# Full-width output tiles and a transposed remainder in a fused attention and FFN kernel

**What was changed.** In three of four token blocks the output projection is cut differently (512 columns per row tile, and the other 128 columns made transposed), and the order in which its pieces are mixed with the P·V work is a fixed list of names.

## The chip, the cores and the metric

One core of one Trainium2 chip. The metric is device time in microseconds (us). The time of a kernel is the median of its runs; "fast" is a state of a run in which the clock was not lowered, and all repeated runs here were fast (experiment 1 was run once, so its state is not known). Ratios are the mean time of one kernel's fast runs over the mean of the other's fast runs of the same rounds, so they are not quite the ratio of the medians that are quoted.

## The reference

```python
# x (1, 2048, 640); 32 heads of 192; the last 512 cache positions; all bfloat16
xn = layernorm(x)
q  = (xn @ wq)                         # (2048, 32*192), split in heads
p  = softmax(q @ k[last 512].T * 192**-0.5)
s  = (p @ v[last 512]) as (2048, 6144) @ wo      # (6144, 640)
g  = silu((silu(xn @ w_gate) * (xn @ w_up)) @ w_down)
out = x + s * g
```

## The kernel before

Tokens are handled in four blocks of 512 (`b` = 0 to 3), each of four row tiles of 128 tokens (`qt`). After an FFN part come 16 head pairs. Each pair has a phase of projections and scores, then a stretch in which P·V of this pair alternates with the output projection of blocks two steps back. Most matmuls (9,526 of 11,086 in the record) use only 64 of 128 rows: the contraction of 128 is split in a lower half `lo` and an upper half `hi`, whose matmuls run side by side in the array. They write different banks of PSUM (the memory that the matmuls write to) and exchange banks half way, with a small memset on GpSimd ("turn") as the synchronization.

The parts that matter, with cuts marked by `...`:

```python
    def wo_turn(st, i, qt, turn):            # half of one row tile: 6 matmuls of 320 columns
        ps = st["sc"]
        for j in range(3):
            for k, r in enumerate((lo, hi)):          # lower, upper, lower, upper ...
                n = k ^ turn
                m = nc.tensor.matmul(
                    ps[:, n, 0:HD], OTs[i][r, 3 * qt + j, :], pairs[i // NB]["wo"][r, j, n * HD : (n + 1) * HD],
                    start=(turn == 0 and j == 0), stop=(turn == 1 and j == 2), skip_group_check=True,
                )
                after(m, st)
        if turn == 0:
            turned(m, st)

    def wo_tile(i, qt):
        ...
        def second():
            sc = st["sc"]
            wo_turn(st, i, qt, 1)
            s_t = sacc[:, t, :].rearrange("p (n d) -> p n d", n=2)
            ...
                nc.vector.tensor_tensor(s_t, s_t, sc[:, :, 0:HD], ALU.add)
        return [first, second]

    def woven(i):                            # the order of one step of a stretch
        (a, b), (w, x, y, z) = (pv(i, 0), pv(i, 1)), (wo_tile(i - 2, qt) for qt in range(4))
        for part in (*a[:2], drop, w[0], *b[:2], w[1], x[0], *a[2:], x[1], y[0], *b[2:], y[1], z[0]):
            part()
        held.append(z[1])
    ...
    for pr in range(NPAIR):
        ... # projections and scores of the four blocks
        for b in range(NB):
            i = pr * NB + b
            if i < 2:
                two(pv(i, 0), pv(i, 1))
            ...
                woven(i)
            ...
            if b == 0 and pr + 2 < NPAIR:
                load_k(pr + 2)
            elif b == 1 and pr + 2 < NPAIR:
                load_wq(pr + 2)
            elif b == 2:
                load_wo(pr + 1)
    ... # last pair: P·V, last output projection, one store per row tile
```

All these loads, all DMA transposes and nearly all stores are issued from one queue, that of SyncE (SPq in the profile), in program order.

The softmax here doesn't subtract the row's maximum and nothing guards it: scores larger than these inputs give would overflow.

## Time and profile before

| | before |
|---|---|
| median, runs beside the changed kernel | 922.53 us (922.36 to 923.72, 6 runs) |
| span of the profiled execution | 920.66 us |
| TensorE busy | 99% of the span |
| period of a head pair, pairs 3 to 14 | 47.03 us, 12 times |

A word on reading. PE is TensorE's matmuls and PEld its weight loads; DVE is VectorE, ACT ScalarE, POOL GpSimd; SPq is SyncE's queue of DMA issues. In a group line the columns are line, engine, operation, output and inputs with their size, count, then busy time and mean duration of one, then the idle time before them. In a timeline a line is start, length, engine, line, operation and count, with idle time and what ended it in brackets; neighbours of one kind are run together. The timeline of SyncE's queue before:

```profile
905.17 4.04 SPq L670 DMA_DIRECT2D out_dram<-x_r  x8
909.30 7.95 SPq L670 DMA_DIRECT2D out_dram<-ob  x7
918.04 0.33 SPq L663 DMA_DIRECT2D out_dram<-ob  x1
```

Every row tile has a store of its own; the last issue is 1.6 us after the last group of matmuls starts (916.45 us).

The view of TensorE's waits lists only two, both before the first head pair, and both for DVE (total us, times, longest).

```profile
PE gu L225 <- DVE zero_t L174: 1.2, 1, 1.2
PE tp L326 <- DVE xn L262: 0.2, 1, 0.2
```

### The profile page before, as it was taken

The numbers are of one execution on the slowest core, as the hardware profiler recorded it, in microseconds if no ns is written. First come the engines' busy times: TensorE is split into PE (matmuls) and PEld (weight loads), VectorE is DVE, ScalarE is ACT, GpSimd is POOL, SyncE is SP. The second block draws the span as 40 slices with busy tenths as digits, with TensorE's granted clock in tenths as the row PEclk, the third lists the DMA queues.
The fourth block names the chain that finished last, engine by engine and source line by source line (L and its number), as shares of the span: only waits on it lengthen the run. The fifth ranks groups of instructions, "written<-read, shape, count | busy, mean of one in ns | idle before, by whom it ended". The sixth has DMA issues, their size and how long they took to land.

```text
span 920.7 us, 25767 instructions
## 1 busy us (share of the span) xinstructions
PE 914.6 (99%) x11086; PEld 625.9 (68%) x11102; DVE 575.8 (63%) x847; ACT 474.6 (52%) x850; POOL 101.9 (11%) x390
## 2 busy tenths in 40 slices
PE   9999999999999999999999999999999999999998
PEld 5455556575858585868686767676777777676666
DVE  6343331467676767676766667676767676767656
ACT  4222222556464646565556565655555555556461
POOL 0000000000000000000000000000000000002978
PEclk9999999999999999999999999999999999999999
DMA  9330510045644444435536262635271717163524
GB/s 308 64 75 18 110 35 1 1 78 89 92 74 85 82 83 83 79 87 70 97 62 104 60 108 53 113 48 119 44 122 36 130 37 126 31 129 86 130 62 142
DMA packets 243762, 77.18 MB, mean 84 GB/s; under 512 B 224576, under 2 KB 243648, under 8 KB 243648
## 3 DMA queue, kind: packets, MB, share of 16 engines
q1 hardware_dynamic: 243216, 75.14, 41.9%
q8 instruction: 87, 1.43, 0.7%
q10 hardware_dynamic: 432, 0.39, 0.2%
q14 instruction: 27, 0.22, 0.1%
HBM read 39.45 MB, written 2.62 MB: 46 GB/s over the span
## 4 chain that ended last, share of the span: by engine, by line
PE 98%; POOL 0%; DMA 0%; DVE 0%; issue 0%; POOLq 0%; ACT 0%; DVEq 0%
PE mm L440 22%; PE sc L576 19%; PE sc L454 18%; PE mm L479 16%; PE sc L277 11%; PE mm L299 6%; PE sc L548 2%; PE mm L531 2%; POOL ob L636 0%; PE gu L277 0%; PE mm L548 0%; PE mm L312 0%; DMA x_t<-in_A_x_dram 0%; PE sc L479 0%; PE sc L531 0%
## 5 line engine op out<-in xcount | busy, mean ns | idle before, releaser
L458 ACT ACTIVATE p_t<-sc 128x1024 bf16<-128x1024 f32 x254 | 253.0, 1023 | 128.2 <-PE sc L454 128.2
L445 DVE TENSOR_REDUCE qT<-mm 128x512 bf16<-128x1024 f32 x189 | 231.1, 1223 | 95.3 <-PE mm L440 92.8
L509 ACT ACTIVATE O_b<-mm,r 128x192 bf16<-128x192 f32 x486 | 165.0, 422 | 180.8 <-issue 156.3
L440 PE MATMUL mm<-xnT,wq_p 64*128 64x512 bf16 x1890 | 240.2, 376 | 0.0
L601 DVE TENSOR_TENSOR sacc<-sacc,sc 128x640 f32<-128x640 f32 x200 | 164.2, 821 | 87.0 <-PE sc L576 87.0
L576 PE MATMUL sc<-wo_p,OT_b 64*128 64x320 bf16 x2592 | 217.3, 296 | 0.0
L454 PE MATMUL sc<-qT,khat 64*128 64x512 bf16 x1524 | 198.2, 376 | 0.0
L479 PE MATMUL mm<-V_p,p_t 64*128 64x193 bf16 x3520 | 186.4, 242 | 0.0
L479 PEld LDWEIGHTS <-p_t 64*128 64x128 bf16 x3584 | 162.9, 93 | 12.1
L440 PEld LDWEIGHTS <-wq_p 64*128 64x128 bf16 x1890 | 105.7, 94 | 93.4 <-issue 0.5
L576 PEld LDWEIGHTS <-OT_b 64*128 64x128 bf16 x2592 | 140.4, 94 | 21.4
L454 PEld LDWEIGHTS <-khat 64*128 64x128 bf16 x1536 | 85.9, 94 | 79.8
L564 POOL MEMSET turn_t<- 128x1 f32 x328 | 32.5, 99 | 691.9 <-PE mm L479 469.7
L285 DVE TENSOR_TENSOR hT<-sc,sg 128x512 bf16<-128x512 f32 x46 | 31.7, 691 | 83.7 <-ACT sg L284 83.7
L284 ACT ACTIVATE sg<-sc 128x512 bf16<-128x512 f32 x46 | 27.3, 597 | 73.4 <-PE sc L277 71.9
L277 PE MATMUL sc<-xnT,wg_sb 128*128 128x512 bf16 (+1 forms) x248 | 59.5, 353 | 0.7
L277 PE MATMUL sc<-xnT,wu_sb 128*128 128x512 bf16 (+1 forms) x259 | 60.2, 354 | 0.1
L299 PE MATMUL mm<-wd_sb,hT 128*128 128x320 bf16 x384 | 56.6, 299 | 0.0
L498 DVE RECIPROCAL r<-mm 128x4 f32<-128x4 f32 x124 | 22.6, 182 | 46.9 <-PE mm L479 36.1
L299 PEld LDWEIGHTS <-hT 128*128 128x128 bf16 x384 | 37.6, 98 | 18.9
L277 PEld LDWEIGHTS <-wu_sb 128*128 128x128 bf16 x285 | 27.1, 98 | 26.9 <-issue 0.2
L277 PEld LDWEIGHTS <-wg_sb 128*128 128x128 bf16 x285 | 27.1, 98 | 22.7
(69 smaller groups left out, 374.9 us busy)
## 6 DMA issues: line engine op xcount, KB each, us to landing
wo_p<-in_A_wo_dram SPq DMA_DIRECT2D x16, 480.0 KB, 4.4
K_p<-in_A_k_cache_dram SPq DMA_DIRECT2D x32, 192.0 KB, 3.3
V_p<-in_A_v_cache_dram SPq DMA_DIRECT2D x32, 192.0 KB, 3.0
wq_p<-in_A_wq_dram SPq DMA_DIRECT2D x64, 80.0 KB, 3.0
wq_p<-in_A_wq_dram SPq DMA_DIRECT2D x16, 160.0 KB, 3.4
x_r<-in_A_x_dram SPq DMA_DIRECT2D x16, 160.0 KB, 4.7
x_t<-in_A_x_dram SPq DMA_DIRECT2D x14, 160.0 KB, 3.0
OT_b<-O_b SPq DMA_TRANSPOSE x124, 3.0
```

Of the source, the lines that this page charges most:

```text
L277: nc.tensor.matmul(out, w_sb[:, c, f * P : (f + 1) * P], xnT[:, c, qc], start=(c == 0), stop=(c == NC - 1),)
L285: nc.vector.tensor_tensor(hTs[b][:, f, :], u, sg[:], ALU.mult)
L299: nc.tensor.matmul(dn[:, 0:HD], hTs[b][:, f, ti * P : (ti + 1) * P], wd_sb[:, f, cols], start=(f == 0), stop=(f == NF - 1),)
L440: nc.tensor.matmul(q_ps[:, h, :], pairs[pr]["wq"][r, c, j * P : (j + 1) * P], xnT[r, c, b * 512 : (b + 1) * 512], start=(c == 0), stop=(c ...
L445: nc.vector.reduce_sum(qTs[i][:, j, :], q_ps[:, :, :].rearrange("p h n -> p n h"), axis=AX.X)
L454: nc.tensor.matmul(sc[:, h, :], khat[r, j, ks], qT[r, j, :], start=(j == 0), stop=(j == 2))
L458: nc.scalar.activation(p_t[:, :, :], sc[:, :, :], ACT.Exp, scale=scale)
L479: m = nc.tensor.matmul(acc[:, k, h * 256 : h * 256 + Dh + 1], Ps[i][kc][r, h, qt * P : (qt + 1) * P], V_p[r, kc, h, 0 : Dh + 1], start=(p ...
L509: nc.scalar.activation(O_b[:, qt, h, :], a_k[:, h, 0:Dh], ACT.Copy, scale=r[:, k, h, :])
L564: st["turn"] = nc.gpsimd.memset(turn_t[:], 0.0)
L576: m = nc.tensor.matmul(ps[:, n, 0:HD], OTs[i][r, 3 * qt + j, :], pairs[i // NB]["wo"][r, j, n * HD : (n + 1) * HD], start=(turn == 0 and j ...
L601: nc.vector.tensor_tensor(s_t, s_t, sc[:, :, 0:HD], ALU.add)
```

## The change

The intent: pieces of 512 columns instead of 320, so fewer instructions for the same columns. A row tile of 640 output columns becomes 512 columns (`MAIN`), two row tiles sharing one PSUM buffer, and the last 128 columns of a whole block are made the other way round: the weights stand still, the 512 tokens move, and the result is transposed. Sums, gate and x of those columns are kept transposed too; three DMA transposes turn them back at the end. Block 3 stays as it was. A list of names sets the order of the units.

```diff
+    def wo_rest(ps, i, r=slice(0, P), first=True, end=True):
+        for j in range(3):
+            nc.tensor.matmul(
+                ps.rearrange("p (t q) -> p t q", q=P), pairs[i // NB]["wo"][r, j, MC:D],
+                OTs[i][:, :, :].rearrange("p (t j) q -> p j t q", j=3)[r, j, :, :],
+                start=(first and j == 0), stop=(end and j == 2),
+            )
...
+    def wo_units(i):
...
+        def rest():
+            sc = sc_tile()
+            for n, r in enumerate((lo, hi)):        # three lower, then three upper
+                wo_rest(sc[:, n, :], i, r)
+            for n in range(2):
+                add_sum(pr + n, s_t[:, b, :], sc[:, n, :])
+        if b == MB:
+            return [unit([(qt, cols) for cols in HALVES]) for qt in range(4)]
+        return [unit([(2 * h + k, MAIN) for k in range(2)]) for h in range(2)] + [[rest]]
...
-    def woven(i):
-        (a, b), (w, x, y, z) = (pv(i, 0), pv(i, 1)), (wo_tile(i - 2, qt) for qt in range(4))
-        for part in (*a[:2], drop, w[0], *b[:2], w[1], x[0], *a[2:], x[1], y[0], *b[2:], y[1], z[0]):
-            part()
-        held.append(z[1])
+    FIRST = """0a0 0b0 0a1 0b1 0e0 1b0 1a0 1b1 2a0 1a1 2w0 2a1 2w1 2x0 2b0 2x1 3x0 2b1 3x1 3a0 2y0 3a1
+        3b0 3y0 3w0 3b1 3w1"""
+    LATER = """0a0 0b0 0y0 0x0 0a1 0x1 0w0 0b1 0w1 1x0 1a0 1x1 1b0 1w0 1a1 1w1 1z0 1b1 1z1 1y0 2b0 1y1
+        2y0 2b1 2x0 2a0 2x1 3w0 2a1 3w1 2w0 3a0 2w1 3b0 3a1 3y0 3x0 3b1 3x1"""
...                                                # end of the kernel
-        for k in range(2):
-            wo_last(b, 2 * q2 + k, G)
+        last_rows(b, slice(2 * q2, 2 * q2 + 2), G, sc_tile)
+        if q2:
+            last_rest(b, V if b else G, mm_tile if b else sc_tile)   # ends in a DMA transpose
         if more:
             pv_full(i + more[0], more[1])
+        if q2:
+            store_block(b)                                           # 640 KB in one store
+    last_rest(2, V, sc_tile)
...
```

In a name such as `2w1`, 2 is the step, `a` and `b` are P·V units, `w`, `x`, `y`, `z` output units (`y` is the transposed piece in blocks 0 to 2, `e` a projection), and the last digit the half of the unit. The down-projection of the FFN was cut in the same way.

## The prediction

> **What bounds the kernel now.** I read the page first (engine shares, chain, groups), then the timeline inside one head pair, then the waits.
>
> ```profile
> PE 914.6 (99%) x11086; PEld 625.9 (68%) x11102; DVE 575.8 (63%) x847; ACT 474.6 (52%) x850; POOL 101.9 (11%) x390
> ...
> PE 98%; POOL 0%; DMA 0%; DVE 0%; issue 0%; POOLq 0%; ACT 0%; DVEq 0%
> ...
> L440 PE MATMUL mm<-xnT,wq_p 64*128 64x512 bf16 x1890 | 240.2, 376 | 0.0
> L576 PE MATMUL sc<-wo_p,OT_b 64*128 64x320 bf16 x2592 | 217.3, 296 | 0.0
> L454 PE MATMUL sc<-qT,khat 64*128 64x512 bf16 x1524 | 198.2, 376 | 0.0
> L479 PE MATMUL mm<-V_p,p_t 64*128 64x193 bf16 x3520 | 186.4, 242 | 0.0
> ```
>
> TensorE is busy 99% of the span, it is 98% of the chain that ended last, and its large groups were never idle before an instruction (the last column is 0.0). But busy time of pipelined matmuls is no rate, so I took starts from the timeline: first in the stretch of projections and scores, then in the stretch where P·V and the output projection alternate.
>
> ```profile
> 404.46 0.83 PE L454 MATMUL sc<-qT,khat 64*128 64x512 bf16 x6
> 405.11 1.26 PE L440 MATMUL mm<-xnT,wq_p 64*128 64x512 bf16 x10
> 406.19 1.48 PE L454 MATMUL sc<-qT,khat 64*128 64x512 bf16 x12
> ```
>
> ```profile
> 477.62 0.85 PE L479 MATMUL mm<-V_p,p_t 64*128 64x193 bf16 x16
> ...
> 478.29 0.99 PE L576 MATMUL sc<-wo_p,OT_b 64*128 64x320 bf16 x12
> 478.59 0.10 POOL L564 MEMSET turn_t<- 128x1 f32 x1 [0.57 <-PE mm L479]
> 478.91 0.82 DVE L601 TENSOR_TENSOR sacc<-sacc,sc 128x640 f32<-128x640 f32 x1 [0.66 <-PE sc L576]
> ...
> 479.10 0.85 PE L479 MATMUL mm<-V_p,p_t 64*128 64x193 bf16 x16
> ```
>
> The first column is the start. The matmuls use 64 of 128 rows, so a lower-half and an upper-half matmul run together; I call such a pair a slot. Ten 512-column matmuls take 406.19 - 405.11 = 1.08 us: 216 ns a slot. Sixteen of 193 columns take 478.29 - 477.62 = 0.67 us: 83 to 84 ns. Twelve of 320 take 479.10 - 478.29 = 0.81 us: 135 to 136 ns.
>
> Now one head pair in slots: projection 60 and scores 48 of 512 columns, P·V 128 of 193, output projection 96 of 320: 108 x 0.216 + 128 x 0.083 + 96 x 0.136 = 23.3 + 10.6 + 13.0 = 46.9 us. The view of stretches puts the period, start of one pair's P·V phase behind the next one's projections included, at:
>
> ```profile
> 442.45:489.48 47.03, 47.03 (x669) 33.92 (x664) 32.62 (x46) 26.80 (x49) 2.38 (x24) 1.00 0.45 81
> ```
>
> 47.03 us at full granted clock. So there is no waiting left inside a pair, and any order of the units can at best win about 0.1 us a pair. The first FFN part is as dense: in the chain, twelve down-projection matmuls take 69.21 - 67.58 = 1.63 us, 136 ns each.
>
> ```profile
> 67.58 1.63 PE mm L299 x12
> 69.21 2.16 PE sc L277 x10
> ```
>
> **What the Trainium skill says.** "TensorE: Matmul & The Clock Gate", section "Back-to-back issue gap", gives N/2.4 + 2.5 ns for a warm matmul of N columns: 82.9, 135.8 and 215.8 ns for 193, 320 and 512. The trace agrees with all three. Of that, only the 2.5 ns belongs to the matmul and not to its columns. The same page, section "The mechanism", says of row-tiled matmuls that their starts and ends are monotone in program order, "strict FIFO, no reordering"; only weight loads are pulled ahead. "PSUM — Partial Sum Buffer", section "Engine vs sequencer instructions", also says that matmuls start and complete in program order, weight loads apart. The trace of before neither shows nor contradicts it: lower and upper half alternate there in every case, so nothing ever stood blocked in front of a free half. "TensorEngine Tiling (Array Packing)", section "Gotcha 1: PSUM Pressure", says that different row tiles cannot use one PSUM bank at once. That explains the turn memsets on POOL, and why the new 128-column piece has two banks and two adds.
>
> **The change part by part.**
>
> Removed. In blocks 0 to 2 an output row tile was two pieces of 320 columns; it is one of 512, and the remaining 128 columns are made transposed, with 512 tokens as the moving side. Per pair and block, 24 slots of 320 become 12 + 3 slots of 512. Both are 7680 columns, so only 9 x 2.5 = 22 ns are saved; times 48 (16 pairs, 3 blocks) 1.1 us. FFN down: 96 matmuls of 320 become 60 of 512 in three blocks, 3 x 36 x 2.5 ns = 0.3 us. One hole of some 0.08 us in the first pair's P·V stretch may close. Sum: -1.4 us.
>
> Added on TensorE. The transposed piece is emitted by a helper that is called once per half with the three contraction steps inside it. The changed kernel's instruction order therefore has three lower-half matmuls, then three upper-half ones; all other row-tiled work alternates. That order gives 164 places where a matmul follows one of the same half, and before had none: four in each of 41 pieces (pairs 0 to 12 with 3 blocks, pair 13 with 2; the others use all 128 rows). With in-order starts the lower ones start at 0, 216 and 432 ns, and the first upper one only after the third, at about 452, though its half has been free since about 20 ns. So the upper half falls 432 ns behind. Before a piece the lower half may already run ahead, but by no more than one 193-column slot less the 20 ns between starts, 63 instead of 20 ns, so from the second piece on 432 - 43 = 389 ns are lost. 41 x 0.389 + 0.04 = 16.0 us. Nothing hides it, since TensorE is the path.
>
> Moved, beside the path. DVE adds per block were 4 x 0.82 = 3.3 us; now two of 1024 columns and two of 512. For 1024 I take the 1.22 us of the q sums (same PSUM width), for 512 the 0.69 us of the FFN gate: 3.8 us. Over three blocks +1.6 us on 32.6 us of DVE in a period of 47: no bound. ScalarE does the same work. Twelve more DMA transposes of x fall in the FFN part, where the DMA row shows idle slices; three transposes of output come before the block stores at the end.
>
> Waits that the new order could bring, as distance against need. A turn needs the matmul's tail of 0.16 us (its 242 ns less the slot of 83), the memset of 0.10 and the semaphores, about 0.4 us; the shortest distance between the two turns of a unit is one half of a P·V unit, 0.66 us. A score buffer behind the transposed piece needs 2 x 0.69 + 0.2 = 1.6 us and has three units, 1.96 us. The tightest P·V buffer (second unit of step 0, reused in step 1) needs the reciprocal 0.18, four ScalarE copies 1.4 and 0.3 of tails, 1.9 us, and has 2.1. All fit, the last narrowly; the lag makes the distances longer. So +0.
>
> Sum: 922.8 - 1.4 + 16.0 = 937.4, less rounding: 937.3 us (+1.6%).
>
> **Rivals.**
> (1) The halves queue separately, and the upper three run beside the lower three. For it: the order of the units was tuned with a model, which should have priced such a loss. Against it: both page statements, and that one instruction stream feeds both halves. It would make 922.8 - 1.4 = 921.4 us.
> (2) One matmul per half can wait outside the queue: then only the third blocks, 216 ns less per piece, 41 x 0.17 = 7 us lost: 928.5 us.
> (3) A new wait binds: the P·V buffer above, or DVE behind the two adds. At 0.1 us for each of 4 blocks in 14 pairs it would be 5 us more. Against it: the distances above.
> (4) The end: block 2's store of 640 KB waits for the last output transpose and stands ahead of the final row tiles in the queue. Stores of 160 KB land in 1.9 us and the transposes in some 3, and the last matmuls of block 3 run some 6 us after block 2's: hidden, or up to 2 us.
>
> **Range and chances.** In-order starts get 0.8, with 936 to 939.5 from small waits and the end; partial blocking 0.08, separate queues 0.12. The range 928 to 940.5 holds the first two. Two per cent of 922.8 is 18.5 us: the gain ever possible is 1.4, so faster is 0.01; slower than 941.2 needs in-order starts and some 4 us of rivals 3 or 4: 0.05.
>
> **What would show each step.** Starts of the six matmuls of one transposed piece: 0, 216, 432, then 452, 668, 884 if in order; pairs 20 ns apart if rival 1 holds. The period should be 47.03 + 3 x 0.389 - 0.07 = 48.1 us; 46.95 under rival 1. The slots should keep 83, 136 and 216 ns. FFN should end 0.3 us earlier. New PE waits on DVE or ACT would show rival 3; a longer stretch from the last matmul (4.0 us now) to the end rival 4. The prediction is wrong if the period stays at 47 or grows by a cause other than these six matmuls.

## More of the kernel before

```profile
194.45 2.60 SPq L512 DMA_TRANSPOSE OT_b<-O_b  x2
197.23 1.22 SPq L102 DMA_DIRECT2D K_p<-in_A_k_cache_dram  x2
198.50 3.39 SPq L512 DMA_TRANSPOSE OT_b<-O_b  x2
201.98 2.81 SPq L113 DMA_DIRECT2D wq_p<-in_A_wq_dram  x5
204.90 3.44 SPq L512 DMA_TRANSPOSE OT_b<-O_b  x2
```

In the first stretch, transposes of P·V outputs (which the output projection needs as its weights) share the queue with loads for later pairs.

## The result and the profile after

| | before | after |
|---|---|---|
| median | 922.53 us | 925.94 us (925.50 to 927.23, 6 runs) |
| ratio, after over before | | 1.0036, 95% interval 1.0024 to 1.0049 |
| span of the profile | 920.66 us | 923.99 us |

The changed kernel is correct and 0.4% slower. By the threshold of 2% that is "same", the class that the prediction gave 0.94, but 937.3 us and the range from 928 to 940.5 were wrong. From the page of the changed kernel: busy times, the chain by engine, and groups.

```profile
PE 914.2 (99%) x10172; PEld 538.7 (58%) x10193; DVE 594.7 (64%) x844; ACT 473.8 (51%) x841; POOL 91.0 (10%) x302
...
PE 97%; DMA 1%; SPq 1%; DVE 0%; issue 0%; POOLq 0%; POOL 0%; DVEq 0%
...
L619 PE MATMUL sc<-wo_p,OT_b 64*128 64x512 bf16 (+1 forms) x1608 | 180.5, 345 | 0.4 <-DMA OT_b<-O_b 0.4
L499 PE MATMUL mm<-V_p,p_t 64*128 64x193 bf16 x3520 | 179.2, 242 | 0.0
...
L632 DVE TENSOR_TENSOR s_m<-s_m,sc 128x1024 f32<-128x1024 f32 x82 | 100.2, 1221 | 49.3 <-PE sc L619 43.0
...
L632 DVE TENSOR_TENSOR s_t<-s_t,sc 128x512 f32<-128x512 f32 x82 | 56.3, 686 | 18.2 <-PE sc L587 16.8
```

There are 914 fewer matmul records (11086 and 10172; a few are missing, the weight loads fall by 909), TensorE is still the path, and the adds last what was predicted. New in the chain are 1% of DMA and 1% of SyncE's queue. The stretches of one head pair (start and end, its length, busy time of TensorE, of its weight loads, of DVE, ACT and POOL, then the granted clock):

```profile
491.54:538.50 46.96, 46.96 (x613) 29.08 (x611) 33.97 (x45) 26.83 (x49) 1.79 (x18) 1.00 0.46 82
```

46.96 us, 0.07 *less* than before, where the prediction had 48.1. So the predicted lag of the transposed pieces is not there. The timeline around one such piece:

```profile
480.39 0.82 PE L587 MATMUL sc<-OT_b,wo_p 64*128 64x512 bf16 x6
...
481.04 0.84 PE L499 MATMUL mm<-V_p,p_t 64*128 64x193 bf16 x16
...
481.33 1.40 DVE L632 TENSOR_TENSOR s_t<-s_t,sc 128x512 f32<-128x512 f32 x2
```

Six matmuls of 512 columns take 481.04 - 480.39 = 0.65 us, three slots of 216 ns. Their single starts in the trace are 0, 10, 216, 226, 432 and 442 ns: in pairs, though the program has three lower ones and then three upper ones.

Where did the 3.3 us of the span come from, then? I cut both traces at the first score matmul of each pair (all in us; "last pair" is from the start of its score phase to the end of the last matmul):

| stage | before | after | difference |
|---|---|---|---|
| start to first score phase (x, layernorm, FFN) | 168.18 | 169.08 | +0.90 |
| first pair | 41.67 | 42.84 | +1.17 |
| second pair | 45.96 | 45.88 | -0.08 |
| pairs 3 to 14 | 564.36 | 563.66 | -0.70 |
| pair 15 | 47.26 | 47.17 | -0.09 |
| last pair | 49.50 | 49.41 | -0.09 |
| last matmul to the end | 3.73 | 5.94 | +2.21 |
| span | 920.66 | 923.99 | +3.33 |

So the middle gains 1.0 us in all, and the change loses more at its two ends. The first row has two parts: up to the first matmul of the FFN's down-projection it is +1.17 us (38.21 and 39.38), and from there to the first score phase -0.27 us (129.97 and 129.70). SyncE's queue at the end of the changed kernel:

```profile
908.79 1.42 SPq L738 DMA_TRANSPOSE x_b<-o_t  x1
911.58 0.39 SPq L757 DMA_DIRECT2D out_dram<-x_b  x1
912.07 1.80 SPq L738 DMA_TRANSPOSE x_b<-o_t  x1
917.52 0.38 SPq L757 DMA_DIRECT2D out_dram<-x_b  x1
917.99 2.28 SPq L764 DMA_DIRECT2D out_dram<-x_b  x3
920.36 0.51 SPq L752 DMA_DIRECT2D out_dram<-x_b  x1
```

Read it from top to bottom as one queue. Block 1's transpose is issued at 908.79. The next entry, block 1's store, has to wait until that has landed, and is issued at 911.58. Only then can block 2's transpose follow, at 912.07, though its input was ready at 908.45. Block 2's store waits for it in turn until 917.52, and the row tiles of block 3 stand behind that store. The last matmuls start at 917.56, and the last issue is 2.8 us later, where it was 1.6 before.

And SyncE's queue with TensorE in the first stretch (timeline of the changed kernel):

```profile
197.65 1.22 SPq L107 DMA_DIRECT2D K_p<-in_A_k_cache_dram  x2
...
200.66 2.85 SPq L118 DMA_DIRECT2D wq_p<-in_A_wq_dram  x5
...
200.89 0.82 PE L619 MATMUL sc<-wo_p,OT_b 64*128 64x512 bf16 x6 [0.36 <-DMA OT_b<-O_b]
...
203.61 2.56 SPq L532 DMA_TRANSPOSE OT_b<-O_b  x2
...
208.22 0.40 PE L587 MATMUL sc<-OT_b,wo_p 64*128 64x512 bf16 x2 [0.33 <-DMA OT_b<-O_b]
```

Two matmul groups now wait for a DMA transpose (and a third, at 203.10, for 0.08 us), and the transposes are issued behind loads for later pairs. The chain of the same stretch has the second wait as a step:

```profile
203.61 4.56 DMA OT_b<-O_b
...
208.22 0.83 PE sc L587 x6
```

Idle 0.36, 0.08 and 0.33 us, and 0.16 us of a matmul's modelled tail (its 376 ns less the slot of 216) counted as busy before each, make 1.25 us; less the 0.04 us that the new pieces of two blocks save, that is the 1.17 us within 0.04.

### The profile page after: what moved, and what is told of

Same layout as the page of the kernel before. It is cut to its first block, busy times and chain, and to the rows that moved or that the text cites. A ratio compares the mean times of both kernels' runs of the same rounds, so it can differ in the third digit from the quotient of the medians.

```text
span 924.0 us, 23739 instructions
## 1 busy us (share of the span) xinstructions
PE 914.2 (99%) x10172; PEld 538.7 (58%) x10193; DVE 594.7 (64%) x844; ACT 473.8 (51%) x841; POOL 91.0 (10%) x302
## 4 chain that ended last, share of the span: by engine, by line
PE 97%; DMA 1%; SPq 1%; DVE 0%; issue 0%; POOLq 0%; POOL 0%; DVEq 0%
PE mm L460 22%; PE sc L474 18%; PE sc L619 16%; PE mm L499 16%; PE sc L282 11%; PE mm L321 6%; PE sc L587 3%; PE mm L551 2%; PE sc L579 2%; PE mm L579 1%; DMA x_t<-in_A_x_dram 1%; DMA OT_b<-O_b 0%; PE gu L282 0%; PE mm L330 0%; SPq L118 0%; PE sc L551 0%
## 5 line engine op out<-in xcount | busy, mean ns | idle before, releaser
L619 PE MATMUL sc<-wo_p,OT_b 64*128 64x512 bf16 (+1 forms) x1608 | 180.5, 345 | 0.4 <-DMA OT_b<-O_b 0.4
L499 PE MATMUL mm<-V_p,p_t 64*128 64x193 bf16 x3520 | 179.2, 242 | 0.0
L460 PEld LDWEIGHTS <-wq_p 64*128 64x128 bf16 x1890 | 95.8, 94 | 108.0 <-issue 0.7
L632 DVE TENSOR_TENSOR s_m<-s_m,sc 128x1024 f32<-128x1024 f32 x82 | 100.2, 1221 | 49.3 <-PE sc L619 43.0
L474 PEld LDWEIGHTS <-khat 64*128 64x128 bf16 x1536 | 78.0, 94 | 87.8
L619 PEld LDWEIGHTS <-OT_b 64*128 64x128 bf16 x1608 | 78.6, 94 | 43.5 <-DMA OT_b<-O_b 1.8
L605 POOL MEMSET turn_t<- 128x1 f32 x246 | 24.4, 99 | 699.0 <-PE mm L499 494.2
L632 DVE TENSOR_TENSOR s_t<-s_t,sc 128x512 f32<-128x512 f32 x82 | 56.3, 686 | 18.2 <-PE sc L587 16.8
L632 DVE TENSOR_TENSOR s_o<-s_o,sc 128x640 f32<-128x640 f32 x52 | 42.7, 822 | 15.9 <-PE sc L619 14.8
L321 PE MATMUL mm<-wd_sb,hT 128*128 128x512 bf16 (+1 forms) x238 | 46.5, 347 | 0.1
```

Source lines behind the costliest of these rows:

```text
L321: nc.tensor.matmul(dn, at, by, start=(f == 0), stop=(f == NF - 1))
L460: nc.tensor.matmul(q_ps[:, h, :], pairs[pr]["wq"][r, c, j * P : (j + 1) * P], xnT[r, c, b * 512 : (b + 1) * 512], start=(c == 0), stop=(c ...
L474: nc.tensor.matmul(sc[:, h, :], khat[r, j, ks], qT[r, j, :], start=(j == 0), stop=(j == 2))
L499: m = nc.tensor.matmul(acc[:, k, h * 256 : h * 256 + Dh + 1], Ps[i][kc][r, h, qt * P : (qt + 1) * P], V_p[r, kc, h, 0 : Dh + 1], start=(p ...
L619: m = nc.tensor.matmul(ps[:, k, 0 : cols.stop - cols.start], OTs[i][r, 3 * qt + j, :], pairs[i // NB]["wo"][r, j, cols], start=(turn == 0 ...
L632: nc.vector.tensor_tensor(to, to, ps, ALU.add)
```

## The experiments

**Theories.** On the missing lag: (a) the halves have queues of their own, with no order between them; (b) the chip looks ahead only a few instructions, and the three waiting lower matmuls are within its reach; (c) starts are in order after all, and the order that the chip sees is not the program's, because something before it interleaves the halves. On the lost 3.3 us: the end's queue order, the first stretch's loads, or scatter from run to run.

### 1. Short upper matmuls between long lower ones

In the piece that decides, the equal length of the two halves could still hide the order. So the upper half of the changed kernel's transposed pieces was cut into matmuls of 256 columns.

```diff
+        n = 2 if r == hi else 1
         for j in range(3):
-            nc.tensor.matmul(
-                ps.rearrange(...), pairs[i // NB]["wo"][r, j, MC:D], ...[r, j, :, :],
+            for k in range(n):
+                ts = slice(k * 4 // n, (k + 1) * 4 // n)
+                nc.tensor.matmul(
+                    ps.rearrange(...)[:, ts, :], pairs[i // NB]["wo"][r, j, MC:D], ...[r, j, ts, :],
```

> The changed kernel, with each upper-half matmul of the transposed 128-column piece cut into two of 256 tokens, so that length tells the halves apart in the trace; the program still has three lower ones first, then six upper ones. Theory A (the halves are served separately): the starts of a piece show 256-column matmuls between the 512-column ones, the first within about 25 ns of the first lower one, and the piece still takes about 3 x 216 = 650 ns; time 925.9 + 41 x 3 x 2.5 ns = 926.2 us. Theory B (starts in program order): no 256-column start before the third 512-column one, some 450 ns after the first; then the gap-free pieces of the changed kernel would need another explanation.

Measured: 926.21 us (one run), correct. The view of groups by form over one pair shows both lengths (the window holds three whole pieces and cuts a fourth, so not 1 to 2; no record of these pieces is missing):

```profile
L590 PE MATMUL sc<-OT_b,wo_p 64*128 64x512 bf16 x12 | 3.2, 376 | 0.0
L590 PE MATMUL sc<-OT_b,wo_p 64*128 64x256 bf16 x21 | 2.9, 269 | 0.0
```

and the starts of the nine matmuls of the piece at 245.69 us in the trace, in ns, are

```
512 columns (lower):    0            216            432
256 columns (upper):       25   134       243  353       462  571      next unit: 648
```

The first upper matmul stands behind all three lower ones in the program, and starts 25 ns after the first of them. The two lengths rule out that labels were mistaken. By itself that leaves theory (c) open: a compiler could have interleaved the halves. The same trace decides it. From piece to piece the upper half, with three instructions more, falls back by some 7.5 ns: its first start comes 3 ns after the lower one's at 205.67 us, 25 ns in the piece above, 115 ns at 433.54 us. The order of starts changes with it: above, the second upper matmul starts before the second lower one (134 and 216 ns); at 433.54 us it starts after it (224 and 216 ns). An order fixed before the run does not drift. So theory (c) falls: matmuls of the free half overtake waiting ones of the other. How far is not yet said.

### 2. Long blocks of one half in the kernel before

To find the depth, every row-tiled loop of the kernel before was turned over: first all lower matmuls of a unit, then all upper ones. That makes blocks of five (projection), three (scores, output) and eight (P·V).

```diff
@@ q_rows
-        for c in range(NC):
-            ...
-            for h, r in enumerate((lo, hi)):
+        for h, r in enumerate((lo, hi)):
+            ...
+            for c in range(NC):
@@ scores, and likewise wo_turn
-        for j in range(3):
-            for h, r in enumerate((lo, hi)):
+        for h, r in enumerate((lo, hi)):
+            for j in range(3):
@@ pv: both heads' four steps of one half, then the other half
-            for kc in range(KC):
-                for n, r in enumerate((lo, hi)):
+            for n, r in enumerate((lo, hi)):
+                for h, kc in ((h, kc) for h in range(2) for kc in range(KC)):
```

(The wait for the turn goes to the first matmul of each half, so that it stays free of races.)

> The kernel before, with every row-tiled group blocked by half: 5 lower then 5 upper projection matmuls, 3 and 3 for scores and for each turn of the output projection, 8 and 8 for each turn of P.V. Same matmuls, same buffers. Theory A (halves served separately, at least 8 matmuls deep): 922.5 us within 2 us, period of a pair 47.0 us. Theory B (starts in program order): each group of n and n takes almost 2n - 1 slots instead of n; summed over all groups about +390 us, some 1315 us. A limited look-ahead of some matmuls would lie between, and would show first in the groups of 8.

Measured: 949.52 us (949.03 to 949.91, 4 runs), ratio 1.0287 (1.0273 to 1.0301), correct. One pair:

```profile
302.00:350.84 48.84, 48.84 (x670) 37.02 (x666) 32.72 (x46) 26.77 (x49) 2.36 (x24) 1.00 0.44 78
```

1.81 us a pair are lost. In-order starts would cost, by the prediction's rule carried over, 2(n - 1) slots for a block of n instead of n: 12 x 3 x 0.216 (projection) + 16 x 1 x 0.216 (scores) + 16 x 6 x 0.083 (P·V) + 32 x 1 x 0.136 (output) = 23.6 us a pair. Entirely separate queues would cost nothing. It is neither. The single starts say how far the chip sees. After a common start, in a block of five the lower ones start at 0, 227 and 442 ns, and the first upper one at 235: with the second lower one, while three lower ones still wait. In a block of eight the lower ones start at 0, 83, 169, 251 and 334, and the first upper one at 342: with the fifth, while again three still wait. A matmul passes at most three waiting ones of the other half. The timeline also has a case that can be seen without single records:

```profile
169.51 0.38 PE L454 MATMUL sc<-qT,khat 64*128 64x512 bf16 x1
169.53 0.38 PE L440 MATMUL mm<-xnT,wq_p 64*128 64x512 bf16 x1
```

The first score matmul starts before a projection matmul that stands ahead of it in the program. So theory (b) holds, with a depth. The lag of the upper half is made anew after each turn that both halves wait for; that this makes up the whole of the 1.81 us was not separated, nor whether the limit counts matmuls alone or their weight loads too.

### 3. Blocks of at most four

If the reach is three, a block of up to four of one half must cost nothing. The second kernel again, with the projection in blocks of 4 and 1 and P·V in blocks of 4.

```diff
@@ q_rows
-        for h, r in enumerate((lo, hi)):
-            for c in range(NC):
+        for c, h, r in [(c, h, r) for cs in (range(4), (4,)) for h, r in enumerate((lo, hi)) for c in cs]:
@@ pv
             for n, r in enumerate((lo, hi)):
-                for h, kc in ((h, kc) for h in range(2) for kc in range(KC)):
+                for kc in range(KC):
```

> The kernel before, blocked by half as e2, but with at most four matmuls of one half in a row (projection 4 and 4, then 1 and 1; P.V 4 and 4; scores and output projection 3 and 3). Theory A4 (a matmul can start ahead of at most three waiting ones of the other half, read from e2, where the first upper one started with the second of five lower ones and with the fifth of eight): nothing is lost, 922.6 us within 1 us and a period of 47.0 us. Rival (any blocking loses something, for instance through the turns, which wait for the later half): between 924 and 950 us, roughly half of the 27 us of e2.

Measured: 923.38 us (923.12 to 923.47, 4 runs), ratio 1.0008 (0.9994 to 1.0021).

```profile
302.40:349.43 47.03, 47.03 (x666) 34.55 (x664) 32.63 (x46) 26.81 (x50) 2.36 (x24) 1.00 0.43 82
```

The period is that of the kernel before to the digit, and so are all twelve of pairs 3 to 14 (564.36 us). The loss of 1.81 us is gone. That confirms the reach from the other side. The first two pairs were 0.46 and 0.22 us longer in its one profile, the last 0.21. In the first one a matmul waits 0.24 us for a DMA transpose (203.91 us), which with its tail of 0.16 is 0.40 of the 0.46; the others stay open.

### 4. The transpose ahead of the store

In the changed kernel, block 1's store was put behind block 2's transpose.

```diff
-        if q2:
+        if q2 and b == 0:
             store_block(b)
     last_rest(2, V, sc_tile)
+    store_block(1)
```

> The changed kernel, with the output transpose of block 2 issued before the store of block 1 instead of after it. Theory T (the 2.2 us that the end is longer is the queue: block 1's store waits for its own transpose, so block 2's transpose is issued late, and block 2's store and all later stores wait behind it): from the last matmul's end to the end of the span 3.8 to 4.2 us instead of 5.95, time 925.9 - 2.0 = 923.9 us. Rival U (the end is longer because 640 KB stores are large and the DMA engines are full): no change, 925.9 us.

Measured: 923.73 us (922.94 to 925.04, 5 runs), ratio to before 1.0007 (0.9993 to 1.0021), where the change as it was had 1.0036. SyncE's queue:

```profile
909.77 2.67 SPq L738 DMA_TRANSPOSE x_b<-o_t  x2
912.54 2.69 SPq L757 DMA_DIRECT2D out_dram<-x_b  x2
915.67 3.73 SPq L764 DMA_DIRECT2D out_dram<-x_b  x3
920.13 0.33 SPq L752 DMA_DIRECT2D out_dram<-x_b  x1
```

Both transposes go out back to back, and block 2's store no longer stands at the very end: last matmul to span's end is 4.16 us instead of 5.94. The stores are as large as in the change, so the rival that blamed their size falls. The single cause "queue order" explains 1.78 of the 2.21 us; 0.4 us of the end stay unexplained.

### 5. The loads of the first pair behind its stretch

```diff
             if int(name[0]) > step:
-                loads(step)
+                if pr:
+                    loads(step)
                 step += 1
             units[name[:2]][int(name[2])]()
+        for b in range(0 if pr else 3):
+            loads(b)
```

> The changed kernel, with the loads of later weights in the first pair's P.V stretch issued after that stretch instead of inside it. Theory L (the 1.2 us lost in the first pair are waits for transposed outputs, because the K and query-weight loads stand ahead of the transposes in the queue): first pair from the start of P.V to the start of the next one's 40.6 to 40.8 us instead of 41.76, time 925.9 - 1.1 = 924.8 us. Rival M (the distance from P.V to the output projection of the same block is too short in the first pair's order, whatever else the queue holds): at most 0.4 us better, 925.5 us or more.

Measured: 924.51 us (924.09 to 924.80, 5 runs), ratio to before 1.0017 (1.0004 to 1.0029). The first pair is 42.04 us long in its profile, against 42.84 and, in three other profiles that kept the change's first stretch, 43.90, 43.56 and 44.06. TensorE's idle time behind transposes in this pair was 0.77 us in the change's profile and 1.83, 1.49 and 2.00 in those three; here it is 0.32. So the loads held it up for the most part. One wait is left, though no load now stands ahead of that transpose:

```profile
199.80 0.82 PE L619 MATMUL sc<-wo_p,OT_b 64*128 64x512 bf16 x6 [0.32 <-DMA OT_b<-O_b]
```

That much speaks for the rival M of the expectation, an order of units that leaves too little distance. And by the measure that the expectation named, from the start of one P·V phase to the next, the pair came to 41.54 us, not 40.6 to 40.8. Part of the excess is the wait above; the rest lies in the second pair, which went from 45.88 to 46.46 us because K of the third pair now comes late. The view of DVE's waits has

```profile
DVE ssum L151 <- DMA KT<-K_p: 1.8, 1, 1.8
```

The wait was in part moved, not removed.

### 6. Both ends together

Experiment 4, and in the first stretch a milder form of 5: K is loaded one step later, the other loads after the stretch, and row tiles 2 and 3 of block 0 (`2x`) half a unit later (`3x` and `3a` change places too).

```diff
-    FIRST = """... 2w1 2x0 2b0 2x1 3x0 2b1 3x1 3a0 2y0 3a1
-        3b0 3y0 3w0 3b1 3w1"""
+    FIRST = """... 2w1 2b0 2x0 2b1 2x1 3x0 3a0 3x1 2y0
+        3a1 3b0 3y0 3w0 3b1 3w1"""
...
-                loads(step)
+                if pr:
+                    loads(step)
+                elif step == 2:
+                    loads(0)
                 step += 1
...
+        for b in () if pr else (1, 2):
+            loads(b)
```

> The changed kernel with the end of e3 (block 2's output transpose ahead of block 1's store) and a first pair with more room: the output projection of row tiles 2 and 3 of block 0 one half unit later, the K loads one step later, query and output weight loads after the stretch. If the changed kernel's losses are only these two and start-up scatter: first pair 41.6 to 41.9 us and second 45.9 us between score phases (before 41.68 and 45.96), later ones 46.96, from the last matmul's end to the end 4.2 us; time 922.5 - 1.4 (saved slots) + 0.4 (end) + 0.1 (first pair) = 921.6 us, the fastest of all. If a cost is still missing from the account: 922.5 us or more.

Measured: 921.95 us (921.84 to 922.51, 5 runs); before beside it 922.53 (922.29 to 923.25, 9 runs); ratio 0.9994 (0.9981 to 1.0006). SyncE's queue in the first stretch and at the end:

```profile
194.12 10.45 SPq L532 DMA_TRANSPOSE OT_b<-O_b  x6
204.62 1.99 SPq L107 DMA_DIRECT2D K_p<-in_A_k_cache_dram  x2
208.47 2.84 SPq L532 DMA_TRANSPOSE OT_b<-O_b  x2
...
906.78 2.66 SPq L738 DMA_TRANSPOSE x_b<-o_t  x2
...
917.14 0.33 SPq L752 DMA_DIRECT2D out_dram<-x_b  x1
```

Six transposes stand ahead of the loads. The first pair is 41.73 us, the second 45.88, the end 4.13. Against before, stage by stage: +0.10, +0.06, -0.08, -0.81, -0.09, -0.09, +0.40, together -0.5 us, and the medians differ by 0.6. It is the fastest median of all the kernels here, but the interval holds 1, so a gain is not shown. TensorE's idle time behind transposes in the first pair is 0.02 us. This run by itself does not separate the order of the units from the place of the loads in the first stretch; beside experiment 5, where 0.32 us were left with no load in the way, it suggests that both had a part. Its time lies between the two that were expected (921.6 us if nothing is missing, 922.5 or more if something is).

### 7. The old order with the new shapes

The new pieces in the order of the kernel before, carried over to them unit by unit.

```diff
-    LATER = """0a0 0b0 0y0 0x0 0a1 0x1 0w0 0b1 0w1 1x0 1a0 1x1 1b0 1w0 1a1 1w1 1z0 1b1 1z1 1y0 2b0 1y1
-        2y0 2b1 2x0 2a0 2x1 3w0 2a1 3w1 2w0 3a0 2w1 3b0 3a1 3y0 3x0 3b1 3x1"""
+    LATER = """0a0 0w0 0b0 0w1 0x0 0a1 0x1 0b1 0y0 1a0 1w0 1b0 1w1 1x0 1a1 1x1 1y0 1b1 1y1 1z0 2a0 1z1
+        2w0 2b0 2w1 2x0 2a1 2x1 2b1 2y0 3a0 3w0 3b0 3w1 3x0 3a1 3x1 3b1 3y0"""
```

> The changed kernel's shapes in all pairs, but the units of pairs 1 to 13 in the order of the kernel before (each block's two P.V units woven with its own output units). Theory Q (the new order is needed: in the old one a P.V buffer returns after 1.96 us with 1.9 us of work on it, and the wider score buffers keep DVE 1.22 us at a time): period 47.3 to 47.8 us instead of 46.96, time 925.9 + 13 x 0.3 to 0.8 = 930 to 936 us. Rival (the order is worth nothing, only the shapes count): period 46.96 us, 925.9 us.

Measured: 937.46 us (937.22 to 937.97, 4 runs), ratio to before 1.0161 (1.0146 to 1.0177). The period is 47.88 us, 0.91 more than with the new order and just above the 47.3 to 47.8 expected, as the time is above 930 to 936; 13 pairs make 11.8 us, and the medians differ by 11.5. The timeline shows one of the holes:

```profile
347.45 1.35 ACT L529 ACTIVATE O_b<-mm,r 128x192 bf16<-128x192 f32 x4 [0.31 <-DVE r L518]
...
347.87 0.83 PE L619 MATMUL sc<-wo_p,OT_b 64*128 64x512 bf16 x6
...
348.86 0.57 PE L499 MATMUL mm<-V_p,p_t 64*128 64x193 bf16 x9 [0.16 <-ACT O_b L529]
```

Six matmuls of three slots are over at 347.87 + 0.65 = 348.52, but the next P·V unit starts at 348.86: its buffer is one that ACT has not yet copied out. This pair has one more such wait, 0.40 us at 384.32; with the tail of 0.16 before each, the two make 0.88 of the 0.91 us. So the new pieces do bring a new wait, and the order that came with them takes it away. It is a needed part of the change, not an ornament. (That this total is close to the predicted 937.3 is chance: the cause is another.)

## Why the prediction was wrong

The step that failed is the one named "Added on TensorE": "With in-order starts the lower ones start at 0, 216 and 432 ns, and the first upper one only after the third", and its sum of 41 x 0.389 + 0.04 = 16.0 us. In its place the runs show pairs 10 ns apart and a loss of zero. A matmul starts ahead of up to three waiting ones of the other half (experiments 1 to 3), and a piece has only three. In-order starts had been given 0.8. The prediction had itself noted that the trace of before could not show the point, as the halves alternated everywhere; the weight came from two general sentences, and experiments 1 and 2 refute them for the starts of row tiles.

Point by point, the rest:

- **Saved slots: right.** The period was predicted at 46.95 under rival 1, and is 46.96. The 27 slots that a pair has less save 0.07 us, 2.6 ns each. The last pair gained 0.09. The FFN gained its 0.3 us: from the first down-projection matmul to the first score phase it is 129.97 us in all three profiles with the old shapes and 129.69 to 129.70 in all six with the new ones. What scatters lies before that: the first down-projection matmul starts between 38.2 and 39.7 us, late and early ones with both shapes. So the rest of the +0.90 in the table, +1.17, is not put down to the change.
- **Rival 1** (separate queues) gave the right number for the middle and is wrong in kind: under it, experiment 2 would have cost nothing. **Rival 2** (limited reach) was right in kind, with 0.08 and a reach of one instead of three. With three it costs nothing here.
- **Rival 3** (a new wait): none in the middle with the order that came with the change; with another order it is real and binds (experiment 7), on a P·V buffer, the kind that the prediction called the tightest. In the first stretch a wait of this kind was missed: the prediction looked there only for a hole that might close, and did not follow the transposes through SyncE's queue. That cost 1.17 us in this profile, and 1.9 to 2.4 us in the three others that kept this stretch.
- **Rival 4** (the end, "hidden or up to 2 us"): 2.21 us, just above its upper edge. The mechanism is the queue it named; that block 1's store also holds up block 2's transpose was not seen.
- **DVE**: predicted +1.6 us a period, measured 33.97 - 32.62 = +1.35, with adds of 1221 and 686 ns as predicted. No bound, as said.

With 0 in place of the 16.0 us, the prediction's sum would be 921.4 (from the 922.8 that it took for before). The end adds 2.21 us, and the first stretch 1.17 in this profile but 1.9 to 2.4 in the three others: 924.8 to 926.0, an estimate, and the measured median is 925.94. Experiment 6 fits: with both taken away its median is 4.0 us below the change's, more than the 1.17 + 2.21 of the one profile. So 1.17 is probably a low draw of a cost of about 2 us, and what the same profile lost at its start is taken for scatter; four profiles don't settle more.

## What to carry to other kernels

When an engine is 99% busy and a period is the sum of its slots, changing the shape of matmuls with the same number of columns wins only the few ns that belong to each instruction (here 2.6); look for what it costs at the first and last stage, where there is no other work to hide a wait. There, read the one in-order DMA queue from top to bottom: put a transpose that something waits for ahead of stores and prefetches that nobody waits for yet, and look at what then comes later (K in experiment 5). And row-tiled halves needn't alternate one by one in the program: up to four of one half in a row cost nothing here.

## What the Trainium skill lacked or had wrong

- "TensorE: Matmul & The Clock Gate", section "The mechanism" (starts and ends in program order, "strict FIFO, no reordering"), and "PSUM — Partial Sum Buffer", section "Engine vs sequencer instructions" (matmuls start in program order): wrong for the starts of row-tiled matmuls in two halves. An upper one started 25 ns into a piece, ahead of two lower ones that precede it in the program and started at 216 and 432 ns; a score matmul started at 169.51 us, a preceding projection matmul at 169.53.
- No page gives the depth of this look-ahead. Here a matmul passed at most three waiting ones: the first upper one started with the second of five and with the fifth of eight. Blocks of up to four kept the period of 47.03 us; blocks of five and eight, with three among them, made it 48.84.
